# Local attention into a squared-ReLU MLP: a split weight load and an earlier release of later loads

## The chip, the cores and the metric

The kernel runs on one core of one Trainium2 chip. The metric is device time in microseconds. The program is one fused kernel: attention with a local window and a few global keys, then a two-layer MLP on its output. Data moves between HBM and the core's SBUF by DMAs, which are issued by three sequencers here: SP (sync), ACT (scalar) and POOL (gpsimd). POOL's DMAs convert float32 to bfloat16 on the way.

## The reference

```python
scores = (1/sqrt(64)) * q @ k.T  - slope[h] * dist      # 4 batches, 8 heads, 768 positions, head size 64
keep   = (key < 8) | (0 <= query - key < 96)            # 8 global keys, window of 96
a      = softmax(where(keep, scores, -1e9))
x      = (a @ v) as [3072, 512]                          # heads side by side
h      = maximum(x @ w_in, 0)                            # w_in  512 x 2048
out    = (s * h*h + b) @ w_out                           # w_out 2048 x 512
```

## The kernel before

The 3072 tokens are cut into 12 **granules** of 256 tokens (two blocks of 128), three granules to a batch. For each granule the kernel does the same: transpose queries and keys so that the head dimension lies on the partitions; score products on TensorE (`stage_S`, L435; for granule 1 `block_S`, L526), exponentials on ScalarE (L444, L533) and a multiplication with a mask on VectorE (L451); the product with the values (`stage_A`, L489; for granule 1 `block_A`, L552), whose extra column of ones gives the sums; a division by the sums on VectorE (`normalize`, L459 and L460), which writes the averages into the tile `xn`; a transposition of `xn` into `xT`; the first MLP product (L613) with ReLU (L623) and square (L626, L787); and the second MLP product (L661 for granules 0 to 3; L813 for the pairs of later granules, in a form with seven half-size products).

The order of the work on every engine is written out by hand (`manual_schedule`): the opening from L1001 to L1127, then calls of `step`, each of which puts the scores of the next two units, the value products of two units and some MLP work one after the other. A granule has four units of two heads, so two steps.

Loads. The first granule's q and k come by SP and ACT. All others are issued by POOL, in one queue, in program order: q and k blocks (`nat` tiles, four of them, used in turn) and v blocks (`vbuf`, one per batch parity), 128 KB each in bfloat16; the weights `w_in_bf` (four quarters of 512 columns, L139, 512 KB each) and `w_out_bf` (four quarters, L145). The opening order at L196 to L215 is: q and k of granule 1's first block, v of granule 0 (two blocks), q and k of granule 1's second block, the first w_in quarter, v of granule 1 (two blocks), three w_in quarters, a small POOL operation, four w_out quarters, granules 2 and 3. In this text W0 to W3 are the w_in quarters, and v2 and v3 are granule 1's value blocks (blocks 2 and 3 of batch 0). Granules 4 and 5 are queued at L1068.

Who needs these: `make_voff(1)` (L390, L391, VectorE) copies value blocks 1 and 2 into a shifted tile `vo`, which `block_A(1, 0)` reads; `p1_mm(0, 0)` and `p1_mm(0, 1)`, the first MLP products of granule 0, read columns 0 to 255 and 256 to 511 of `w_in`; `p1_mm(0, 2)` and `p1_mm(0, 3)` read columns 512 to 1023. The calls are at L1037 to L1050, in this order: `p1_mm(0,0)`, `make_voff(1)`, `block_A(1,0)`, `p1_mm(0,1)`, `block_A(1,1)`, `x_block(1,0)`, `p1_mm(0,2)`.

Granules 6 to 11. Their six loads each (`load_granule`, L115 and L116) are queued in `finish_granule(j)`, four granules ahead (`LEAD`), behind a **gate** (`hold_loads`, L119 to L121): POOL copies one element of a tile, so that it waits until that element has been written, and the loads stand behind it in POOL's queue. Before the change the element is the last of `xT[j]`. For granules up to 3 `xT` is made by TensorE and a copy (`x_by_pe`); for granules 4 and up by two DMA transposes issued by SP (`x_by_dma`, L593), so the gate opens when such transposes have landed. SP's queue also holds the DMA transposes of q and k for granules 4 and up (`qk_by_dma`, L354, four a granule, issued two granules ahead), the shifted value copies by DMA (`load_voff`, L310 and L311) and all stores of the output (L681, L698, L844). The averages `xn` and the tiles `xT` have three buffers each.

Of the kernel before, what the change touches and what calls it, by code (L numbers as in the profile page):

```python
# [17 lines left out]
def kernel(  # L18
# [19 lines left out]
    DM = H * D  # L38
    DF = moe_w_in.shape[1]
    GB = 2  # L40
    GT = GB * P
# [47 lines left out]
    def rows_of(src, b, sb):  # L89
        return src[b, :, sb * P : (sb + 1) * P, :].rearrange("h p d -> p h d")  # L90
# [8 lines left out]
    def load_qk(j, i):  # L99
        b, g = divmod(j, NGR)  # L100
        for n in range(2):
            nc.gpsimd.dma_start(nat_tile(j)[:, n, i, :, :], rows_of(srcs[n], b, g * GB + i))  # L102

    def load_v(j):
        b, g = divmod(j, NGR)
        for sb in range(g * GB, (g + 1) * GB):
            nc.gpsimd.dma_start(vbuf[b % 2][:, sb, :, 0:D], rows_of(v, b, sb))  # L107

    def load_granule(j):
        b, g = divmod(j, NGR)  # L110
        t = nat_tile(j)
        for i in range(GB):
            sb = g * GB + i
            for n in range(2):
                nc.gpsimd.dma_start(t[:, n, i, :, :], rows_of(srcs[n], b, sb))  # L115
            nc.gpsimd.dma_start(vbuf[b % 2][:, sb, :, 0:D], rows_of(v, b, sb))  # L116


    def hold_loads(ap):  # L119
        g = work.tile([P, 1], BF16, name="gate", tag="gate")  # L120
        nc.gpsimd.tensor_copy(g[0:1, :], ap)  # L121
# [15 lines left out]
    def load_w_in(i, n):  # L137
        w = DF // n
        nc.gpsimd.dma_start(  # L139
            w_in_bf[:, :, i * w : (i + 1) * w], w_in_view[:, :, i * w : (i + 1) * w]  # L140
        )
# [53 lines left out]
    nat_tile(0)  # L195
    load_qk(1, 0)  # L196
    load_v(0)
    load_qk(1, 1)
    load_w_in(0, 4)
    load_v(1)  # L200
    for i in range(1, 4):
        load_w_in(i, 4)
    nc.gpsimd.affine_select(
# [60 lines left out]
    xn = {}  # L264
    xT = {}
# [311 lines left out]
    def x_by_pe(j, evac=(nc.vector.tensor_copy, nc.scalar.copy)):  # L577
        t = xT_tile(j)
        nk = KC // len(evac)
        for e, ev in enumerate(evac):  # L580
            ps = ps_h.tile([P, nk, GT], BF16, name="ps_x", tag="psh")
            for kc in range(nk):
                for i in range(GB):
                    c = (e * nk + kc) * P
                    nc.tensor.transpose(
                        ps[:, kc, i * P : (i + 1) * P], xn[j][:, i, c : c + P], ident_bf[:]
                    )
            ev(t[:, e * nk : (e + 1) * nk, :], ps[:])

    def x_by_dma(j):  # L590
        t = xT_tile(j)
        for i in range(GB):
            nc.sync.dma_start_transpose(t[:, :, i * P : (i + 1) * P], xn[j][:, i, :])  # L593
# [347 lines left out]
    def finish_granule(j):  # L941
        if j < X_PE:
            x_by_pe(j)
        else:
            x_by_dma(j)
        if 6 <= j + LEAD < NJ:
            hold_loads(xT[j][0:1, 0, GT - 1 : GT])
            load_granule(j + LEAD)

    def step(s, c0, c1, c2, pool=None, pre=()):  # L950
# [22 lines left out]
        if last:  # L973
            finish_granule(j)
            if SHIFT < j + 2 < NJ:
                load_voff(j + 2)
# [126 lines left out]
    p2_mm(1, 1, FC // 2 + 3, FC)  # L1103
    p2_hold(1, 1)
    finish_granule(2)
    s6 = scores(6)
    split_wsum()
# [12 lines left out]
    make_koff(4)  # L1120
    run(p1[2][6:8])
    finish_granule(3)
    run(scores(8))
    make_voff(4)
# [110 lines left out]
```

## Time and profile before

| | |
|---|---|
| median of 7 runs | 209.77 us (209.16 to 211.85) |
| the profiled execution: own time | 211.41 us |
| the profiled execution: span of its instructions | 209.6 us |
| busy VectorE, ScalarE, POOL | 77%, 61%, 33% of the span |
| POOL's DMA queue (q0) | 74944 packets, 13.11 MB |
| SP's DMA queue (q1) | 33612 packets, 14.13 MB |

Times in the profile are microseconds from the start of the span. PE is TensorE's matmuls, PEld its weight loads, DVE is VectorE, ACT is ScalarE, SP is the sync engine; a name with q (SPq, POOLq) is that engine's sequencer. "A <- B" in a list of waits means that A waited for B, then follow the total, how often, and the longest wait. A bracket at the end of a timeline row is the idle time of the engine ahead of it and what ended it. A row of POOL for a DMA shows the making of its descriptors; the landing of the data is told apart, by the semaphore of the DMA.

### The profile page before, as it was taken

What the parts mean: (1) busy time and instruction counts of PE and PEld (TensorE: products, weight loads), DVE (VectorE), ACT (ScalarE), POOL (GpSimd) and SP (SyncE); (2) the same over time, 40 slices, a digit from 0 to 9 for tenths busy, and PEclk for the clock granted to TensorE, in tenths of its full rate; (3) what the DMA queues carried; (4) which work ended last, traced back from release to release, by engine and by line L of the source; (5) the groups of instructions that cost most, each with busy time, mean ns of one, the idle gap of its engine ahead of it and who ended that gap; (6) DMA issues with size and microseconds to landing.
All of it is one profiled execution on the core that took longest, in us unless ns stands there. A gap on an engine that the chain in (4) does not pass through costs nothing.

```text
span 209.6 us, 5314 instructions
## 1 busy us (share of the span) xinstructions
PE 201.8 (96%) x2183; PEld 160.1 (76%) x2191; DVE 160.8 (77%) x336; ACT 128.7 (61%) x200; POOL 68.3 (33%) x88
## 2 busy tenths in 40 slices
PE   7898999989999999999998999999999999999993
PEld 2676885546876675778887898888898889888883
DVE  7576689996889955799798784599785696737974
ACT  4974668583976638786564667464866665476200
POOL 8964334996827202703800816400000000000000
PEclk9999999999999999999999999999999999999999
DMA  5999999999999999999999999999261210240006
GB/s 162 172 185 206 207 206 172 155 151 137 121 146 123 154 158 171 106 235 241 133 202 128 123 146 211 164 153 135 52 145 62 78 27 3 50 153 0 0 3 200
DMA packets 109780, 28.17 MB, mean 134 GB/s; under 512 B 97820, under 2 KB 108252, under 8 KB 109756
## 3 DMA queue, kind: packets, MB, share of 16 engines
q0 software_dynamic: 74944, 13.11, 84.9%
q1 hardware_dynamic: 33612, 14.13, 41.2%
q10 hardware_dynamic: 1200, 0.59, 1.1%
q8 instruction: 17, 0.28, 0.6%
q14 instruction: 7, 0.06, 0.2%
HBM read 27.26 MB, written 6.29 MB: 160 GB/s over the span
## 4 chain that ended last, share of the span: by engine, by line
PE 77%; DMA 9%; DVE 5%; POOL 3%; ACT 2%; SPq 1%; issue 1%; POOLq 0%; DVEq 0%
PE ps L613 38%; PE ps L813 21%; PE ps L661 8%; DMA xT<-xn 5%; DMA vb<-in_v_dram 4%; PE ps_av L489 4%; PE ps_s L435 4%; POOL nat L102 2%; ACT tmpl L238 2%; DVE wsum L639 1%; SPq L593 1%; POOL vb L107 1%; DVE vo L391 1%; DVE vo L390 1%; DVE pt L451 1%
## 5 line engine op out<-in xcount | busy, mean ns | idle before, releaser
L613 PE MATMUL ps<-xT,w_in_bf 128*128 128x256 bf16 x768 | 90.3, 273 | 0.9 <-DMA xT<-xn 0.9
L623 ACT ACTIVATE gT<-ps 128x512 bf16<-128x512 f32 x96 | 55.8, 598 | 48.6 <-PE ps L613 48.4
L613 PEld LDWEIGHTS <-w_in_bf 128*128 128x128 bf16 x768 | 72.9, 98 | 10.4 <-issue 1.0
L444 ACT ACTIVATE pt<-ps_s 128x1024 bf16<-128x1024 f32 (+1 forms) x44 | 39.3, 946 | 3.4 <-PE ps_s L435 3.4
L661 PE MATMUL ps<-w_out_bf,gT 128*128 128x512 bf16 x120 | 28.7, 380 | 0.5 <-issue 0.2
L813 PEld LDWEIGHTS <-gsum 128*128 128x128 bf16 x256 | 24.1, 98 | 3.7 <-DVE gsum L776 0.5
L451 DVE TENSOR_TENSOR pt<-pt,tmpl 128x1024 bf16<-128x1024 bf16 (+1 forms) x40 | 24.5, 644 | 1.8 <-ACT pt L444 1.6
L787 DVE TENSOR_TENSOR gT<-gT 128x1024 bf16<-128x1024 bf16 x20 | 13.7, 686 | 11.6 <-ACT gT L623 11.6
L661 PEld LDWEIGHTS <-gT 128*128 128x128 bf16 x128 | 11.8, 98 | 13.0
L460 DVE TENSOR_TENSOR xn<-ps_av,rc 128x256 bf16<-128x256 f32 x48 | 20.4, 424 | 1.7
L813 PEld LDWEIGHTS <-gT 128*128 128x128 bf16 x200 | 18.7, 98 | 2.4
L115 POOL DMA_DIRECT2D nat<-in_q_dram x20 | 18.1, 904 | 5.8 <-DMA w_out_bf<-in_moe_w_out_dram 2.9
L116 POOL DMA_DIRECT2D vb<-in_v_dram x20 | 18.0, 900 | 5.9 <-DMA nat<-in_k_dram 2.4
L115 POOL DMA_DIRECT2D nat<-in_k_dram x20 | 17.8, 888 | 6.1 <-DMA w_in_bf<-in_moe_w_in_dram 2.0
L459 DVE RECIPROCAL rc<-ps_av 128x4 f32<-128x4 f32 x48 | 8.7, 182 | 11.6 <-PE ps_av L489 10.2
L489 PEld LDWEIGHTS <-pt 128*128 128x128 bf16 x320 | 14.5, 98 | 3.2 <-DVE pt L451 0.7
L489 PE MATMUL ps_av<-vb,pt 128*128 128x65 bf16 x208 | 15.5, 193 | 0.4 <-DVE pt L451 0.4
L121 POOL COPY gate<-xT 1x1 bf16<-1x1 bf16 x6 | 1.6, 268 | 43.7 <-DMA xT<-xn 39.7
L626 DVE TENSOR_TENSOR gT<-gT 128x512 bf16<-128x512 bf16 x32 | 13.0, 420 | 3.7 <-ACT gT L623 3.3
L813 PE MATMUL ps<-w_out_bf,gsum 128*128 128x256 bf16 x128 | 15.3, 273 | 0.0
L813 PE MATMUL ps<-wsub,gsum 128*128 128x256 bf16 x128 | 15.1, 273 | 0.0
L813 PE MATMUL ps<-w_out_bf,gT 128*128 128x256 bf16 x120 | 13.9, 273 | 0.0
(112 smaller groups left out, 222.2 us busy)
## 6 DMA issues: line engine op xcount, KB each, us to landing
out_dram<-o_q SPq DMA_DIRECT2D x15, 256.0 KB, 2.3
vb<-in_v_dram POOLq DMA_DIRECT2D x24, 128.0 KB, 8.0
nat<-in_k_dram POOLq DMA_DIRECT2D x22, 128.0 KB, 7.2
nat<-in_q_dram POOLq DMA_DIRECT2D x22, 128.0 KB, 7.4
w_in_bf<-in_moe_w_in_dram POOLq DMA_DIRECT2D x4, 512.0 KB, 11.0
w_out_bf<-in_moe_w_out_dram POOLq DMA_DIRECT2D x4, 512.0 KB, 17.3
out_dram<-o_sb SPq DMA_DIRECT2D x4, 256.0 KB, 6.2
out_dram<-o_early SPq DMA_DIRECT2D x4, 256.0 KB, 5.8
```

The source lines that it names most:

```text
L115: nc.gpsimd.dma_start(t[:, n, i, :, :], rows_of(srcs[n], b, sb))
L116: nc.gpsimd.dma_start(vbuf[b % 2][:, sb, :, 0:D], rows_of(v, b, sb))
L444: nc.scalar.activation(pt[:, :, 0:ncol], ps[:, :, 0:ncol], ACT.Exp, scale=QSCALE)
L451: nc.vector.tensor_tensor(pv, pv, m.rearrange("p h a c -> p h (a c)"), ALU.mult)
L460: nc.vector.tensor_tensor(dst, av[:, :, :, 0:D], rc[:].to_broadcast((P, 2, 2, D)), ALU.mult)
L489: nc.tensor.matmul(av[:, i, hi, 0 : D + 1], lhsT=pt[:, hi, c * P : (c + 1) * P], rhs=vv, start=(n == 0), stop=(n == len(terms) - 1),)
L613: nc.tensor.matmul(ps[:, i, :], lhsT=w_in_bf[:, kc, fc * P : (fc + 1) * P], rhs=xT[j][:, kc, :], start=(kc == 0), stop=(kc == KC - 1),)
L623: nc.scalar.activation(gs, ps[:], ACT.Relu)
L626: nc.vector.tensor_tensor(gs, gs, gs, ALU.mult)
L661: nc.tensor.matmul(po[:], lhsT=g_of(j)[:, fc, tb * P : (tb + 1) * P], rhs=w_out_bf[:, fc, :], start=(fc == 0), stop=(fc == FC - 1),)
L787: outs.append(lambda: nc.vector.tensor_tensor(gs, gs, gs, ALU.mult))
L813: nc.tensor.matmul(ps[:, tb, cs], lhsT=stat[:, fc, tb * P : (tb + 1) * P], rhs=mov[:, fc, cs], start=(fc == 0), stop=(fc == NH - 1),)
```

## The change

The first w_in quarter becomes two eighths of 256 columns. Granule 1's two value blocks, which followed the quarter together, now follow one eighth each. In this text E0 and E1 are these eighths. And the gate ahead of the loads of granules 6 to 11 reads the last element of the averages `xn[j]`, which VectorE's last division (L460) of granule j writes, where it read the last element of `xT[j]`.

```diff
-    def load_v(j):
-        b, g = divmod(j, NGR)
-        for sb in range(g * GB, (g + 1) * GB):
+    def load_v(j, blocks=range(GB)):
+        b, g = divmod(j, NGR)
+        for i in blocks:
+            sb = g * GB + i
             nc.gpsimd.dma_start(vbuf[b % 2][:, sb, :, 0:D], rows_of(v, b, sb))
...
     load_qk(1, 1)
-    load_w_in(0, 4)
-    load_v(1)
+    load_w_in(0, 8)
+    load_v(1, [0])
+    load_w_in(1, 8)
+    load_v(1, [1])
     for i in range(1, 4):
         load_w_in(i, 4)
...
         if 6 <= j + LEAD < NJ:
-            hold_loads(xT[j][0:1, 0, GT - 1 : GT])
+            hold_loads(xn[j][0:1, GB - 1, DM - 1 : DM])
             load_granule(j + LEAD)
```

## The prediction

> **What bounds the kernel now.** I read the page's first part, then who TensorE waited for, then the chain of waits in order of time, then the timelines of POOL and SP around the two places found, and last the DMA view of narrow stretches for landing times.
>
> ```profile
> PE 201.8 (96%) x2183; PEld 160.1 (76%) x2191; DVE 160.8 (77%) x336; ACT 128.7 (61%) x200; POOL 68.3 (33%) x88
> ```
>
> TensorE is busy for 201.8 of 209.6 us and its granted clock is full in all 40 slices. No instruction of TensorE changes, so the change can only win what TensorE idles. Who it waited for:
>
> ```profile
> PE ps_w L160 <- DVE idle L150: 1.2, 1, 1.2
> PE ps_av L552 <- DVE vo L391: 0.9, 1, 0.9
> PE ps L613 <- DMA xT<-xn: 0.9, 1, 0.9
> PE ps_s L435 <- ACT qx L325: 0.5, 2, 0.3
> ```
>
> The first is the start of the program and stays. The next two are the only others near 1 us, and each part of the change bears on one of them. The chain of waits shows where they lie:
>
> ```profile
> 7.43 8.96 DMA vb<-in_v_dram
> ...
> 16.49 0.45 DVE vo L390
> 16.93 0.02 issue
> 16.96 0.70 DVE vo L391
> 17.65 0.04 issue
> 17.69 0.61 PE ps_av L552 x15
> ...
> 103.64 1.96 SPq L593
> 105.60 0.06 issue
> 105.66 9.68 DMA xT<-xn
> 115.34 0.14 issue
> 115.48 1.91 PE ps L613 x16
> ```
>
> Columns are start, length, what. First wait: granule 1's first value block lands at 16.39, VectorE makes two copies, and TensorE goes on at 17.69 after 0.94 us idle. Second: granule 6's transposed averages land at 115.34, and TensorE had been idle for 0.88 us. At most 0.94 + 0.88 = 1.8 us, 0.9% of the time, is to be had.
>
> **What the Trainium skill says.** "Perfetto Trace Analysis", DMA Optimizations: splitting a DMA may let part of the work start sooner if the DMA engines are generally idle. Here they are not: between 10 and 20 us the windows view gives a DMA share of 1.58 (packets overlap), so a split only reorders. "DMA: Bandwidth & Descriptors", Issuing engines are not separate DMA queues: DMAs of sync, scalar and gpsimd end on the same 16 engines and interleave. The trace agrees: from 104 to 116 us the loads' queue and SP's queue moved 3933 and 3595 packets side by side. Same page, Queues, rings and completion order: each engine takes turns between the queues by packet and consumes a ring in order. So a transpose released together with loads has to share, and it also stands behind SP's own earlier stores.
>
> **Part 1, the split quarter.** POOL's queue before is W0 (512 KB), v2, v3, W1, W2, W3; after, E0 (256 KB), v2, E1, v3, W1 and so on. One DMA is added, nothing else.
>
> Issue: the quarter's descriptors took 0.80 us on POOL, so one more costs POOL about 0.8 us. It is hidden: POOL runs far ahead of the data. It stops to wait for landings, always for the DMA eight issues back:
>
> ```profile
> 14.39 0.74 POOL L145 DMA_DIRECT2D w_out_bf<-in_moe_w_out_dram  x1 [1.12 <-DMA w_in_bf<-in_moe_w_in_dram]
> 16.67 0.74 POOL L145 DMA_DIRECT2D w_out_bf<-in_moe_w_out_dram  x1 [1.54 <-DMA vb<-in_v_dram]
> 17.40 0.89 POOL L115 DMA_DIRECT2D nat<-in_k_dram  x1
> 19.56 0.88 POOL L115 DMA_DIRECT2D nat<-in_q_dram  x1 [1.27 <-DMA w_in_bf<-in_moe_w_in_dram]
> ```
>
> Without that cover (a queue run dry) it would cost its 0.8 us.
>
> Data: W1, W2, W3 land 2.5 us apart (19.28, 21.87, 24.39), so a quarter drains in 2.5 us and an eighth in about 1.25. Packets of half the size may cost more (128 KB in small packets take 0.9 us a block, 3.6 us for what a quarter moves in 2.5), so between 1.1 and 1.5 each; I take 1.3, making everything behind later by 0.1 us (bounds: 0.3 earlier, 0.5 later).
>
> First value block: ahead of it goes an eighth less, so it lands at 16.39 - 1.2 = 15.2. VectorE is free from 14.8; its copies (0.45 + 0.70) end at about 16.4. TensorE ends what is ahead (L526) at 16.6 and no longer waits: +0.94 us there, up to 17.1. There it needs E1, which takes the value block's old place: 16.4 to 16.9, in time.
>
> What is late next: columns 512 to 1023 of w_in, which is W1. TensorE used it from 19.86; 0.94 earlier is 18.92, but W1 lands at 19.28 + 0.1 and is seen 0.1 later: 19.5. So 0.94 is gained and 0.57 given back: **0.37 us** is left (0 if W1 comes 0.5 later, 0.75 if it comes 0.3 earlier). The next transfer in this order is the last w_out quarter, landed at 34.57; its first product starts at 35.19, so a gain of 0.37 and a delay of 0.1 still fit in 0.62.
>
> **Part 2, the earlier gate.** The gate is a one-element copy on POOL (0.18 us) with six loads queued behind it; only its release changes. Gates of granules 2 and 3 opened at 52.15 and 62.26 by VectorE's copies; the divisions end at 50.55 and 60.16. Nothing comes of it: loads in front of them land up to 61.21 and 70.76, so new ones only queue longer. Cost 0.
>
> Granules 4 to 7 differ:
>
> ```profile
> 82.01 0.18 POOL L121 COPY gate<-xT 1x1 bf16<-1x1 bf16 x1 [11.99 <-DMA xT<-xn]
> 97.83 0.73 POOL L121 COPY gate<-xT 1x1 bf16<-1x1 bf16 x1 [10.00 <-DMA xT<-xn]
> 115.46 0.18 POOL L121 COPY gate<-xT 1x1 bf16<-1x1 bf16 x1 [11.71 <-DMA xT<-xn]
> 127.36 0.18 POOL L121 COPY gate<-xT 1x1 bf16<-1x1 bf16 x1 [6.03 <-DMA xT<-xn]
> ```
>
> The divisions end at 77.43, 90.02, 102.41 and 118.31, so the four gates open about 4.6, 7.8, 13 and 9 us sooner. No transfer on SP waited for these loads, so an early landing wins nothing by itself. What changes is which loads run beside which transposes:
>
> - Granule 4's transposes (issued 77.45, landed 81.96, used 85.20) had the engines to themselves after 80.2; now they share with granule 8's loads. About 1.9 us of their packets becomes some 4: landed near 84, still in time.
> - Granule 5's (91.20, 97.71, used 99.64) ran beside granule 8's loads; now those end near 90 and granule 9's begin near 92. Landed 97 to 99.5, in time by a little.
> - Granule 6's (103.64, 115.34) are the stalled ones. Before, granule 9's six loads were issued from 98.50 to 103.76, all ahead. After, those have mostly drained and granule 10's start draining near 104.4 (gate 102.5, 1.5 us from issue to first packets), together with the transposes. Work from 92 on, at rates of packets alone: six loads at 0.87 us (POOL's spacing, which they keep), 5.2; on SP's queue three stores at 0.6, six transposes at 0.62 (1030 packets in the microsecond after 127, some 530 a transpose) and the value copy at 0.9, 6.4. Shared, the queues reach about 0.87 of their rates alone (after 103, some 680 load packets of 1200 and 260 of 850 a us), so 11.6 us becomes 13.4, to 105.4; then 1.4 us of stores and 1.25 of transposes at half share, 6 us: 111.5. Before, their packets ended near 112.9 and landed at 115.34. So about 1 us sooner: landed near 114.4, bounds 112.5 and 118.5, since this balance is the difference of large numbers.
> - Granules 7 and 8: used at 131.63 and 146.09, landed at 127.24 and about 142; nothing near.
>
> TensorE would ask for granule 6 at 114.60 - 0.37 = 114.23, and with landing at 114.4 plus 0.14 starts at 114.54 instead of 115.48: 0.94 us earlier in all. From there TensorE runs to 206.4 with no wait over 0.05 us, so all of it reaches the end.
>
> **Sum.** 209.6 - 0.94 = 208.7 of span. The profiled execution's own time was 211.41, 1.8 us around its span; the median of seven is 209.77. I take the difference off the median: **208.8 us**.
>
> **Rivals.**
> - *Taken back by the transposes.* Granule 6's averages land at 115.3 as before: SP's queue is the limit, whoever shares. Then the first part only makes TensorE wait longer there, since the landing and not TensorE sets the restart: 0 us, 209.8. For it: stores and key transposes stand ahead of them on SP either way. Against: SP's issue follows TensorE's progress.
> - *Loads crowd the transposes (slower).* At granules 5 and 6 the loads now start with the transposes. It decides when granule 5 lands after 99.3 or granule 6 after 115.4; each us beyond costs one us. If granule 10's loads (5.2 us of work) take all turns ahead at granule 6, 115.3 becomes 117 to 119: +1.7 to +3.7, 211.5 to 213.5. For it: a key transpose issued at 82.68 took 6.1 us and granule 6's second one 9.7 us beside loads; alone they take 2.4. Against: granule 9's loads are out of the way by then.
> - *Both waits gone whole.* W1 early and granule 6 in time: -0.75 - 0.88, 208.1.
>
> **How the numbers follow.** Forecast 0.48 (208.3 to 209.4); taken back 0.22 (209.4 to 210.2); crowding 0.23 (210.2 to 213.5, most below 212); both gone 0.07. Faster by over 1% (below 207.7; 1% is about what a measurement can tell from no change) would need more than TensorE idles: 0.04. Slower by over 1% (above 211.9) is over half of crowding: 0.15. Range 207.9 to 211.9.
>
> **What would show it.** Right: the wait of L552 on the vo copies is gone, and a wait of L613 on w_in of about 0.5 us stands near 19 us; gates open near 78, 90, 102 and 118; the wait of L613 on xT near 114 shrinks below 0.5 us. Wrong: a wait on xT near 99 or over 1 us near 115, or w_in later than 19.8.

## The result, and the profile after

| | before | after |
|---|---|---|
| median of the runs on the same chip | 210.16 us (63 runs, 209.16 to 211.85) | 211.21 us (26 runs, 210.18 to 213.21) |
| ratio after to before, 95% interval | | 1.0048 [1.0034, 1.0063] |
| the profiled execution: own time, span | 211.41, 209.6 us | 210.80, 209.0 us |

The change makes the kernel about 1.0 us slower. The two profiled executions alone say the opposite: 209.0 against 209.6 us of span. In both, the own time is the span plus 1.8 us, so the medians stand for spans of 208.4 (before) and 209.4 (after). The execution of before that the prediction read lies near the top of its own runs. The profiled execution of the gate-only kernel in its first run (e2, below) was a slow one, with a granted clock of 0.984, so only e2's ratio of fast runs is used, and traces of that kernel are those of e9.

The page of after, first part:

```profile
PE 202.3 (97%) x2183; PEld 160.3 (77%) x2191; DVE 159.8 (76%) x336; ACT 128.7 (62%) x200; POOL 69.5 (33%) x89
```

TensorE's work is what it was: 2183 matmuls, 202.3 us busy against 201.8. POOL has one instruction more, the added DMA. The list of TensorE's waits in after (total, times, longest):

```profile
PE ps_w L161 <- DVE idle L151: 1.2, 1, 1.2
PE ps L616 <- DMA xT<-xn: 1.1, 1, 1.1
PE ps_s L438 <- ACT qx L328: 0.3, 1, 0.3
PE ps L664 <- issue: 0.2, 1, 0.2
```

All lines of the kernel's body stand three lower, so L616 is L613 of before, and the gate is L122. The wait for the `vo` copies is gone, as forecast; the forecast wait of 0.5 us for W1 near 19 us is not there in this execution. The wait for granule 6's `xT`, forecast below 0.5 us, has grown from 0.88 to 1.07. The timeline of POOL shows that the change does what it says (start, length, in brackets POOL's idle time and its releaser):

```profile
76.30 0.31 POOL L122 COPY gate<-xn 1x1 bf16<-1x1 bf16 x1 [6.42 <-DVE xn L463]
88.97 0.57 POOL L122 COPY gate<-xn 1x1 bf16<-1x1 bf16 x1 [6.82 <-DVE xn L463]
101.67 0.51 POOL L122 COPY gate<-xn 1x1 bf16<-1x1 bf16 x1 [6.82 <-DVE xn L463]
117.76 0.51 POOL L122 COPY gate<-xn 1x1 bf16<-1x1 bf16 x1 [10.20 <-DVE xn L463]
```

The four gates open at 76.3, 89.0, 101.7 and 117.8, within 1.7 us of the forecast. In the chain of waits of after (start, length, what) two landings of `xT` stand, where before there was one:

```profile
91.57 7.14 DMA xT<-xn
98.71 0.05 issue
98.76 1.92 PE ps L616 x16
...
105.53 9.13 DMA xT<-xn
114.67 0.14 issue
114.80 1.91 PE ps L616 x16
```

The first is granule 5, where TensorE idled 0.14 us; the second is granule 6.

### The profile page after: what moved, and what is told of

Read it like the earlier page. It is cut to its first block, busy times and chain, and to the rows that moved or that the text cites. A ratio compares the mean times of both kernels' runs of the same rounds, so it can differ in the third digit from the quotient of the medians.

```text
span 209.0 us, 5316 instructions
## 1 busy us (share of the span) xinstructions
PE 202.3 (97%) x2183; PEld 160.3 (77%) x2191; DVE 159.8 (76%) x336; ACT 128.7 (62%) x200; POOL 69.5 (33%) x89
## 4 chain that ended last, share of the span: by engine, by line
PE 83%; DMA 10%; ACT 4%; issue 1%; DVE 0%; SPq 0%; ACTq 0%
PE ps L616 37%; PE ps L816 19%; PE ps L664 13%; DMA xT<-xn 8%; PE ps_s L438 4%; PE ps_av L492 4%; DMA first<-in_k_dram 2%; ACT pt L447 2%; ACT gT L792 1%; PE ps_t L348 1%; PE ps_s L514 1%; PE ps_t L324 1%; ACT gT L626 1%; PE ps_x L588 1%; PE ps_s L529 1%
## 5 line engine op out<-in xcount | busy, mean ns | idle before, releaser
L616 PE MATMUL ps<-xT,w_in_bf 128*128 128x256 bf16 x768 | 90.4, 273 | 1.3 <-DMA xT<-xn 1.1
L616 PEld LDWEIGHTS <-w_in_bf 128*128 128x128 bf16 x768 | 72.8, 98 | 10.8 <-issue 1.2
L664 PEld LDWEIGHTS <-gT 128*128 128x128 bf16 x128 | 11.8, 98 | 13.2 <-issue 0.3
L629 DVE TENSOR_TENSOR gT<-gT 128x512 bf16<-128x512 bf16 x32 | 12.9, 420 | 3.7 <-ACT gT L626 3.3
L816 PE MATMUL ps<-wsub,gsum 128*128 128x256 bf16 x128 | 15.1, 273 | 0.0
L792 ACT ACTIVATE gT<-gT 128x1024 bf16<-128x1024 bf16 x12 | 12.7, 1057 | 0.4
```

The source lines that it names most:

```text
L616: nc.tensor.matmul(ps[:, i, :], lhsT=w_in_bf[:, kc, fc * P : (fc + 1) * P], rhs=xT[j][:, kc, :], start=(kc == 0), stop=(kc == KC - 1),)
L664: nc.tensor.matmul(po[:], lhsT=g_of(j)[:, fc, tb * P : (tb + 1) * P], rhs=w_out_bf[:, fc, :], start=(fc == 0), stop=(fc == FC - 1),)
L792: nc.scalar.activation(gs, gs, ACT.Square)
L816: nc.tensor.matmul(ps[:, tb, cs], lhsT=stat[:, fc, tb * P : (tb + 1) * P], rhs=mov[:, fc, cs], start=(fc == 0), stop=(fc == NH - 1),)
```

## The experiments

Ratios are to the kernel before on the same chip, with 95% intervals. There are twelve runs: the parts alone, both kernels again, the early gate at one granule or at some, one attempt at a better version, and a half dose.

**e1, the split alone** (the first two hunks of the diff).

> Only the split quarter with the value block between; the gate stays on the landed transposes. Theory A (the split gains what was forecast and a little more, the gate loses more): 0.4 to 1.2 us faster than the kernel before, no wait of block_A's products on the vo copies, waits on xT as in the kernel before. Rival B (the split is what costs, since one more DMA shifts all of POOL's queue): 0.5 to 1.5 us slower. Rival C (the two profiled executions were odd draws, and both parts are near nothing): within 0.3 us.

Measured: 1.0004 [0.9988, 1.0020], median 210.08 us: no difference, as in rival C. Its waits for data, from the list of TensorE's waits:

```profile
PE ps L616 <- DMA xT<-xn: 0.7, 1, 0.7
PE ps L616 <- DMA w_in_bf<-in_moe_w_in_dram: 0.6, 1, 0.6
```

The `vo` wait is gone and a wait for W1 stands in its place: W1 landed at 19.32 and TensorE had waited 0.58 us for it.

**e2, the early gate alone** (the last hunk of the diff), and **e9, the same again**.

> Only the gate on the last division; the first w_in quarter stays whole. Theory A: 1.2 to 2.5 us slower than the kernel before, by longer waits of L613 on xT at granules 5 and 6 (1 to 3 us together). Rival B: within 0.3 us. Rival C: within 0.3 us, and waits on xT as in the kernel before.

> The early gate everywhere, without the split, again, for an undisturbed profiled execution. Theory A (loads 9 beside the key transposes of granule 8 hold SP back, and loads 10 beside granule 6's transposes slow these): 0.4 to 0.9% slower; granule 6's transposes issued 1 us or more later than with the late gate and landed at 115 to 117.5, waits on xT at granules 5 and 6 of 1.5 to 3.5 us. Rival (one odd draw): the same time as before.

Measured: 1.0070 [1.0049, 1.0092] and 1.0033 [1.0013, 1.0053]. Since the split alone changes nothing, the loss is the gate's. In e9 the wait for granule 6's `xT` is 1.11 us.

**e3, before again**, and **e4, after again** (no edit).

> The kernel before itself, for a second profiled execution. Theory A: ratio 1.000 within 0.15%; the wait on xT at granule 6 is smaller than the 0.88 us of the first profile, since the median of the runs lies 1.2 us under that profiled execution. Rival C: the same waits as in the first profile.

> The changed kernel itself, for a second profiled execution. Theory A: 0.3 to 0.7% slower than the kernel before, and waits on xT at granules 5 and 6 of 1.5 to 3 us together, against 1.2 in the first profile. Rival B: waits on xT as before and a later stretch up to 50 us. Rival C: within 0.2% of the kernel before.

Measured: e3 1.0011 [0.9993, 1.0028], e4 1.0064 [1.0040, 1.0089]. The second execution of before has a span of 208.4, and its waits are others than those in the execution that the prediction read:

```profile
PE ps L661 <- DMA w_out_bf<-in_moe_w_out_dram: 0.5, 1, 0.5
PE ps L613 <- DMA xT<-xn: 0.5, 1, 0.5
PE ps L613 <- DMA w_in_bf<-in_moe_w_in_dram: 0.2, 1, 0.2
```

There is no wait for `vo` in it at all: v2 landed at 14.98, not at 16.39. Its chain of waits runs through the weights instead:

```profile
6.68 7.38 DMA w_in_bf<-in_moe_w_in_dram
...
14.34 0.74 POOL w_out_bf L145
15.08 0.18 issue
15.26 19.44 DMA w_out_bf<-in_moe_w_out_dram
34.70 0.04 issue
34.74 4.48 PE ps L661 x20
```

The last `w_out` quarter lands at 34.70 and TensorE has waited 0.50 us for it. In e4, TensorE waits for `xT` three times, 1.8 us in all (0.21, 0.65 and 0.99 at granules 4, 5 and 6).

**e5, e6, e7: before with the early gate at granule 4, 5 or 6 only.**

```diff
-            hold_loads(xT[j][0:1, 0, GT - 1 : GT])
+            hold_loads(xn[j][0:1, GB - 1, DM - 1 : DM] if j == 4 else xT[j][0:1, 0, GT - 1 : GT])
```

(`j == 5` in e6, `j == 6` in e7.)

> The kernel before with the early gate only at granule 4 (the loads of granule 8 released about 5 us sooner); the split is not in. Theory A (loads that drain beside the transposes make these land late, and the end moves by what TensorE then waits): granule 4's transposes land 1.5 to 2.5 us later than with the late gate, just about when they are used; 0 to 0.3 us slower. If only the sum of DMA work counted, the time would be as before or a little better, since these loads are out of the way sooner.

> The early gate only at granule 5 (granule 9's loads 7 us sooner, beside granule 5's transposes instead of ahead of granule 6's). Theory A: granule 5's transposes land about 2 us later (98 to 100), a wait of 0 to 0.7 us there; granule 6's land 2 us sooner and their wait of 0.45 us goes: from 0.4 us faster to 0.3 us slower than before. Rival: any early gate costs, 0.5 us slower or more.

> The early gate only at granule 6 (granule 10's loads 12 us sooner, while granule 9's loads are still where they were). Theory A: both sets of loads meet granule 6's transposes; these land 1 to 3 us later and the kernel is 0.7 to 2.5 us slower than before, with no wait at granule 5. Rival (SP's own order sets the landing whoever shares): within 0.3 us of before.

Measured: 0.9988 [0.9967, 1.0008], 0.9999 [0.9985, 1.0014], 1.0007 [0.9989, 1.0025]. No single gate costs anything that shows; the 0.7 to 2.5 us expected of gate 6 alone did not come. Each profile has at most one wait for `xT`: none in e5, 0.68 us at granule 5 in e6, 0.68 us at granule 6 in e7.

**e8, early at all granules but 6** (condition `j != 6`), and **e11, early at 5 and 6 only** (condition `j in (5, 6)`).

> The early gate at all granules but 6. Theory A: no new loads at granule 6's transposes, so only the waits at granules 4 and 5 are left: 0 to 0.6 us slower than before, and under the time of the early gate everywhere by at least 0.6 us. Rival (the loss comes from granules 4 and 5 alone): as slow as the early gate everywhere, 1 us or more over before.

> The early gate at granules 5 and 6 only. Each alone cost nothing measurable. Theory A (it takes both: loads 9 delay SP's issue of granule 6's transposes, loads 10 then share with them): 0.4 to 0.8% slower, near the early gate everywhere. Rival (losses of granules 4, 5 and 6 simply add): within 0.2%.

Measured: e8 1.0013 [0.9996, 1.0031] with no wait at granule 6; e11 1.0047 [1.0028, 1.0067] with 1.43 us there. So the two early gates at 5 and 6 together make the loss, and either of them alone does not.

**e10, the split and the early gate at all but 6**, as a version that could beat both.

> The whole change, but the gate of granule 6 stays late. Theory A: the loss goes, within 0.25% of the kernel before, granule 6's transposes land near 111.5 and nobody waits for them; all gain left is that of the rare late value block. Rival (the split and the early gate clash elsewhere): still 0.4% or more slower.

Measured: 1.0007 [0.9978, 1.0035]. It is no faster than before. Its ratio is under that of after (1.0048), but the two intervals just touch.

**e12, early everywhere, but three of granule 10's six loads behind a second, late gate** (in `load_granule`).

```diff
+            if j == 10 and i == 1:
+                hold_loads(xT[6][0:1, 0, GT - 1 : GT])
```

> The early gate everywhere, but of granule 10's six loads only the first three are behind it; the last three wait for granule 6's landed transposes. Theory A: half the crowding: granule 6's transposes land between 112.5 and 115, 0 to 0.4% slower than before and faster than the early gate everywhere. Rival (SP's late issue alone makes the loss): as slow as the early gate everywhere.

Measured: 1.0043 [1.0011, 1.0076]. The interval holds both the whole loss and half of it, so theory and rival stay undecided by the time. In its profile granule 6's transposes landed 12.8 us after the division, and TensorE waited 0.49 us.

## Why the prediction was wrong

**The base of part 1 failed.** The term "0.94 is gained and 0.57 given back" was taken from one execution that was not a usual one. Of nine profiled executions whose quarter is whole (e2 left out), v2 landed between 14.9 and 15.1 in seven, with no `vo` wait; only before's first (16.39) and e5's (16.66, a wait of 1.06 us) had that wait. Both own times, 211.41 and 210.66, lie about 1 us above the medians of their kernels (210.16 and 209.59). In the usual execution there is no such wait to win: v2 lands there sooner than the 15.2 that the prediction expected of the change. The split hardly moves the end of the weight loads: the last `w_out` quarter lands at 34.70 in e3 and at 34.57 in e1, and the matmuls after it begin at 34.74 and 34.62. In these two executions the split mainly moves idle time, from 0.23 us at W1 and 0.50 us at `w_out` in e3 to 0.58 us at W1 in e1. The size of the give-back was right (W1 seen near 19.5, landed at 19.32 in e1); the gain that it was taken from belongs to the less usual execution. Why v2 lands late in some executions is not shown. The hint was in the table: an own time of 211.41 beside a median of 209.77. The prediction noted it and took the whole difference off the median anyhow. The way from 208.8 to 211.2 us is then 0.94 of gain that did not come, 1.05 of loss, and 0.4 by which the median of the first seven runs was low. Set against the one execution that it was read from, the forecast span of 208.7 would have looked nearly right (209.0 in after's profile), which is luck: it sets a high execution of before against a rather low one of after.

**Granule 6 in part 2 failed, in the balance of SP's queue.** The failed step is "11.6 us becomes 13.4, to 105.4; then ... 6 us: 111.5" and with it "about 1 us sooner". In after, e4 and e9 the key and query transposes ahead, which this sum had done by 105.4, moved their last packets at 106.3, 108.5 and 107.4, and granule 6's pair of transposes moved its last at 113.9, 115.1 and 114.1, where 111.5 was forecast (packets are counted in the order of SP's queue). That the pair landed at 114.67 in after, near the forecast 114.4, is partly luck. The forecast put 2.9 us between last packet and landing, and 0.6 to 0.8 us passed in these three; and TensorE, 0.87 us ahead of before and not 0.37, asked for the pair at 113.73 and not at 114.23.

Counted from the division, with TensorE 0.37 us ahead, the pair was forecast to land after 12.4 us (from 102.04 to 114.4). It took 13.0 to 13.2 us in after, e4 and e9, and 12.5 to 12.9 in the kernels with no early gate: it came 0.4 us later, not sooner. In the table, the third column counts what SP's queue had yet to move at 104 us of all that the program puts ahead of the pair, and "store" is the output store (L844) just ahead of it. Packets and landings are from the traces; packet sizes tell stores (1024 or 2048 bytes) and transposes (256) apart.

| kernel | early gates | packets ahead of the pair at 104 us | division to landing of the store | store to landing of the pair | sum |
|---|---|---|---|---|---|
| before, e3, e1 | none | 895, 870, 888 | 7.7, 7.8, 6.9 | 5.3, 4.7, 5.9 | 12.9, 12.5, 12.8 |
| e5 | 4 | 1408 | 9.3 | 2.8 | 12.1 |
| e7 | 6 | 756 | 8.0 | 4.7 | 12.7 |
| e6 | 5 | 1538 | 6.5 | 2.6 | 9.1 |
| e8, e10 | all but 6 | 1626, 1807 | 8.7, 8.9 | 1.2, 1.2 | 10.0, 10.1 |
| after, e4, e9 | all | 1513, 1946, 1525 | 9.6, 10.4, 10.4 | 3.6, 2.6, 2.8 | 13.1, 13.0, 13.2 |
| e11 | 5, 6 | 1615 | 10.6 | 2.9 | 13.5 |
| e12 | all, half at 6 | 1523 | 10.1 | 2.7 | 12.8 |

At 92 us some 4000 packets stood ahead of the pair in every kernel (3881 to 4241). With gate 5 early, granule 9's loads then run beside SP's transfers, and SP's queue falls behind. Its packets from 92 to 98 and from 98 to 104 us are in e3

```profile
q1 hardware_dynamic: 2171, 1.42, 109.6%
q1 hardware_dynamic: 1165, 0.29, 34.3%
```

and in e9

```profile
q1 hardware_dynamic: 1517, 1.03, 67.6%
q1 hardware_dynamic: 1255, 0.77, 75.1%
```

A sign of this backlog shows in SP's timeline. In e3 (no early gate):

```profile
99.01 1.25 SPq L354 DMA_TRANSPOSE kx<-nat  x1
100.35 1.30 SPq L354 DMA_TRANSPOSE qx<-nat  x1
101.74 0.53 SPq L681 DMA_DIRECT2D out_dram<-o_sb  x1
102.37 0.43 SPq L844 DMA_DIRECT2D out_dram<-o_q  x1
102.97 3.52 SPq L593 DMA_TRANSPOSE xT<-xn  x2
```

and in e9 (all gates early):

```profile
98.43 1.23 SPq L354 DMA_TRANSPOSE kx<-nat  x1
99.76 3.25 SPq L354 DMA_TRANSPOSE qx<-nat  x1
103.09 0.53 SPq L681 DMA_DIRECT2D out_dram<-o_sb  x1
103.72 0.38 SPq L844 DMA_DIRECT2D out_dram<-o_q  x1
104.21 2.88 SPq L593 DMA_TRANSPOSE xT<-xn  x2
```

The last query transpose ahead of `xT` takes 3.25 us to issue instead of 1.30. It is so in all eight profiles with gate 5 early (3.1 to 3.6 us; in e4 1.88 and 2.39 on the last two) and in none of the five with it late (1.2 to 1.3; there one of the other three took 1.9 to 2.1). When the long issue began, 1650 to 1720 packets of SP's queue were undone; with gate 5 late there were never more than 1023 at the start of any of the four. The long issue is not what held granule 6 up. In e6, e8 and e10 it is there too, and the pair lands 3 us sooner or more. With an empty queue a transpose's first packet moves as its issue ends (granule 11's in e3: 179.20 and 179.21). Granule 6's moved 2.4 to 4.5 us after that in all 13 profiles, when the store ahead of it had drained. And that store landed after the whole pair had been issued: in e9 at 111.9, the issue having ended at 107.09. So the pair stood in its queue and waited for what was ahead.

**Why gates 5 and 6 must be early together.** What happens after 104 us depends on gate 6. The DMA view of 104 to 112 us shows whose packets those are (q0 is POOL's loads, q1 SP's queue; packets, MB, share of 16 engines). In e3 the loads are granule 9's:

```profile
q1 hardware_dynamic: 2117, 1.07, 89.7%
q0 software_dynamic: 2688, 0.34, 68.4%
```

In e9 the rest of granule 9's and then granule 10's:

```profile
q0 software_dynamic: 3144, 0.40, 97.4%
q1 hardware_dynamic: 2092, 0.93, 78.2%
```

In e8 only that rest:

```profile
q1 hardware_dynamic: 3235, 1.44, 126.0%
q0 software_dynamic: 529, 0.07, 12.9%
```

An early gate 5 takes most of granule 9's loads out of this stretch, at the price of the backlog. If nothing follows, SP's queue catches up (3235 packets) and the pair lands early. An early gate 6 fills the stretch with granule 10's loads (2092 packets), and the backlog stays. An early gate 6 alone (e7) finds no backlog. That the loss needs both gates is shown by e6, e7 and e11; that it comes by this way is read from one trace of each. The packets agree with what the Trainium skill, "DMA: Bandwidth & Descriptors", Queues, rings and completion order, says: each DMA engine takes turns between its queues, packet by packet. With load packets beside it, SP's queue moved 2092 packets in these 8 us; with hardly any, 3235.

**Granules 4 and 5** were sized about right: landings forecast near 84 and at 97 to 99.5, measured 83.6 and 98.7 in after, 84.5 and 99.8 in e4. But "in time" was a matter of tenths: of TensorE's waits in after and e4, 0.14 and 0.86 us are at these two. Both signs that the prediction named as proof against it are there: a wait on `xT` near 99, and one of over 1 us near 115 (1.07 in after).

**The sum.** The waits for `xT` add up to 0.88, 0.45 and 0.72 us in before, e3 and e1 (mean 0.7) and to 1.21, 1.85, 1.20 and 1.43 us in after, e4, e9 and e11 (mean 1.4). The difference, 0.7 us or 0.35%, lies inside the intervals of e9 and e11, at the low end of after's, and a little short of e2's and e4's. So it accounts for most of the 1.0 us. In these executions the loss lies in that stretch: from the 1000th matmul, near 97 us, to the last, TensorE took 107.5 to 107.9 us in before, e3 and e1, and 108.5 to 108.9 in after, e4, e9 and e11, 0.9 us more in the mean.

**The rivals.** "Loads crowd the transposes" is what happened, at a lower price (1.0 us, not 1.7 to 3.7), and by another way than it said: granule 10's loads did not take all turns ahead of granule 6's transposes; granule 9's had put SP's queue behind before it came to them, and granule 10's kept it there. The prediction's argument against this rival, that granule 9's loads are out of the way by then, left out what they do on their way. "Taken back by the transposes" asked for no net change and is excluded for after by its interval; it is the fate of the split alone, though there by waits for the weights and not for `xT`. The forecast and "both waits gone whole" rested on the `vo` wait.

**What stays open.** With all gates early the store ahead of the pair lands about 2.7 us later after the division, but the pair then follows it 2.3 us faster than with none; why so much of the backlog is made up is not shown. Nor is it shown by an experiment that the backlog makes the long issue; the two only go together. The row of e5 doesn't fit: its gate 5 is late, and yet 1408 packets stood ahead. And e8 and e10 wait hardly at all for `xT` (0.2 and 0.4 us in their profiles) and are still no faster than before: fewer waits in one execution are not yet time won in the median.

## What to carry to other kernels

Before a wait of one profiled execution is priced, set that execution's own time against the median of the runs: where it lies as high as the wait is long, the wait may belong to that execution alone. Loads that are released earlier do not only share the DMA engines with the transfer that is waited for; they also slow what stands ahead of it in its own queue, so count that backlog too. Before a long issue is blamed for a late landing, see whether the queue still had earlier packets to move when it ended. Where two loads take each other's place beside a critical transfer, moving one away helps only if the next does not follow.

## What the runs showed of the hardware

- A DMA transpose on SP took 1.2 to 1.3 us to issue at most times, and 3.1 to 3.6 us (e6, e8 to e12, after) when it began with some 1700 packets of SP's queue undone. SP issued nothing else meanwhile.
- With SP's queue empty, a transpose's first packet moved as its issue ended (179.20 and 179.21 us in e3). Behind other transfers it moved 2.4 to 4.5 us later (granule 6 in 13 profiles).
- From 104 to 112 us SP's queue moved 2092 packets beside 3144 load packets (e9) and 3235 beside 529 (e8).
- With the same opening, v2 landed either at 14.9 to 15.1 us (seven profiles) or at 16.4 to 16.7 (two).
